# An adaLN block with a long convolution and a gated MLP on one core: one order of accumulation, two stores, one weight form and one activation form moved

## The chip, the cores and the metric

The kernel runs on one core of a Trainium2 chip. Its engines are TensorE (PE in the profile; PEld is its weight loading), VectorE (DVE), ScalarE (ACT), GpSimd (POOL) and SyncE (SP), which here only issues DMAs. ACT issues DMAs too. Each engine runs its own instructions in the order in which the program gives them, and waits on semaphores for the others. The metric is the device time of one execution in microseconds (us).

## The reference

Sequence length S = 2048, width D = 448, hidden width F = 1792, batch 1, all float32.

```python
mod = (silu(c) @ w_mod).reshape(1, 6, 1, -1)          # sa, ca, ga, sb, cb, gb
h = layernorm(q) * (1 + ca) + sa
k_shift = causal_conv4(k, shift_k)                    # per channel
kv = k_shift * v
y = irfft(rfft(kv, 2S) * rfft(ssm_k, 2S))[:S] + kv * ssm_D
x = q + ga * (h * y)
h = layernorm(x) * (1 + cb) + sb
x = x + gb * ((sigmoid(h @ w_gate) * (h @ w_up)) @ w_down)
```

## The kernel before

The first 160 us or so do the long convolution as matrix products, the first normalisation and the gates. Nothing there is touched. The rest is the gated MLP, and it is bound by TensorE.

**Split numbers.** Every operand of a product is split in a high part (the float32 value rounded to the matmul's format, `fp32r`, by a copy on ACT) and a low part (the remainder, by a subtraction on DVE). A product is taken as high·high + low·high + high·low. So each weight form, each activation form and each hidden block costs one ACT instruction and one or two DVE instructions, in this order.

**Rows and hidden groups.** The 2048 rows are four blocks of 512 (n = 0 to 3). The hidden width is seven groups of 256 (k or j = 0 to 6). The gate and up weights of a group come by `load_gu` from DRAM, its down weights by `load_wd`.

**Plain part.** For groups 0 and 1 and row blocks 0 and 1 the products are plain. `plain_half(p, q, n, f)` (L1041 for its matmuls, named gu) makes half a group for a row block: p counts the four pairs (q, n) = (0,0), (1,0), (0,1), (1,1), and f the half. After each half but the first two stands one `down` call, which multiplies the hidden block of the pair before with that group's down weights. Then come the jobs listed in `ends[(p, f)]`. `last_block`, `turn_full` and others run in the middle of a half (`turns`).

**Steps.** After that twelve steps, i = 0 to 11, do the other groups for rows 0 to 1023 and then 1024 to 2047 (and groups 0 and 1 for the latter) with a Strassen-like scheme: seven products per step, with the weight forms A11, S2, S1, S3, A12, A22, S4 (in the order of use) and the activation forms B11, T2, T1, T3, B21, T4, B22. Their matmuls are on L933 (tiles a, b, c in PSUM). Between them stand four `down` calls (`dn`). The second half of the steps (i = 6 and on) works on row blocks 2 and 3.

**Order of the work.** Nothing is planned by a program here: inside the region opened by `tc.manual_schedule()` each engine runs its instructions in the order of the code. A job placed in the lists `ends` or `jobs` (`do("a")`, `do("b")`, … in `step`) stands at that point of the queue of each engine that it uses.

**Names that the change touches.**

- `down(k, n, ks, e)` makes a PSUM tile d from two row tiles (i = 0, 1) with six matmuls each: for each half f of the group (high h, high w), (high h, low w), (low h, high w). The h is the stationary operand. L964 is the matmul, L967 the addition of d to x on DVE. The tile has the tag "y", of which there is one buffer, so the next `down` waits for the addition before it.
- `split_wd_hi` (ACT, L532) and `split_wd_lo` (DVE, L536) make the two parts of the down weights in one of two homes (`wd_of`). `gate_wd` (L526) multiplies them by the gate first. `split_wd_lo` puts the finished pair in the list `kept`.
- `keep_forms(left)` takes stores from that list until `left` remain and issues them on ACT's queue (L543). `w_hi` calls it before its own copy, mostly with `left` = 1. The stored weight forms are read again from step 5 on.
- `w_form` is `w_hi` (ACT, L914) and `w_lo` (DVE, L918); `w_sums` (L894 to L901) makes the sums from the loaded weights on DVE.
- `x_hi` (ACT, L862) and `x_lo` (DVE, L867/L868 or L870) make an activation form in the home that the products read.
- `turn_of` transposes two column tiles of a row block (L851) into a PSUM tile of tag "sa" (one buffer) and copies them out with scale and bias on ACT (`norm_full`, L856). The product tile c of a step has the same tag. `t_sums` (L878 to L885) makes the T sums on DVE from the copied blocks.
- In `step`, u2 (L1209) and u3 (L1216, L1231) are additions on DVE that read the product tiles b and c. b is added to further after u2 has read it.

The part of `step` between the first product and the third, for steps other than 1:

```python
            do("a")
            dn(*((1, 0) if first else (0, 0)))
            lo(0)
            if i < 5 and i != 2:
                gate_wd(JS[i], DVE)
            do("b")
            pb_ = two("t", f"b{i}")
            use(pb_, "S2", "T2", True, True)
            free(2)
            DVE.tensor_add(u2, pb_, c1)
            do("c")
```

Of the kernel before, what the change touches and what calls it, by code (L numbers as in the profile page):

```python
# [79 lines left out]
def adaln_conv_glu_kernel(ctx: ExitStack, tc: tile.TileContext, q, kT, v, ssm, shift, dskip,  # L80
                          wgu, wd, cvec, wmod, c1t, w2t, wat, wbt, out):
    nc = tc.nc
    PE, ACT, DVE, POOL = nc.tensor, nc.scalar, nc.vector, nc.gpsimd
# [11 lines left out]
    late = {}  # L95

    def two(tag, name):

        return ps.tile([P, 2, 512], F32, tag=tag, bufs=2 if tag == "t" else 1, name=name)

    def rows(t):
        return t[:, :, :D]
# [282 lines left out]
    def gate(h, i, y, eng):  # L385

        gg = gt[h, i]
        eng.tensor_mul(pairs(gg), pairs(gg), y)
        gate_add(h, i, gg, eng)
# [57 lines left out]
    def ln2_stats(*tiles, act=()):  # L447

        for i in tiles:
            if i in act:  # L450
                t = two("sa", f"sq{i}")[:, 0, :D] if i > 7 else late["tmp"][:, 29 * C + 32:31 * C + 32]
                ACT.activation(t, x1[:, i], AF.Copy, scale=1.0 / D, accum_out=mv[:, i, 0:1])
                ACT.activation(t, x1[:, i], AF.Square, bias=mv[:, i, 0:1], scale=-1.0, accum_out=mv[:, i, 1:2])
            else:
                st6 = keep.tile([P, nc.vector.BN_STATS_DIM], F32, tag=f"st{i % 2}", name=f"st{i}")
                DVE.bn_stats(st6, x1[:, i])  # L456
                DVE.bn_aggr(mv[:, i], st6)
# [70 lines left out]
    def wd_of(k):  # L528
        return ring["wdk"][k % 2]
# [423 lines left out]
    def down(k, n, ks, e, last=False, split=False, tag="y"):  # L953

        w = wd_of(k)
        g = 4 * n + 2 * e
        pt = two(tag, f"d{k}_{g}")
        for i in range(2):
            ops = []
            for f in range(2):  # L960
                hh, hl = [a1h[ks[f]][:, s] for s in range(2)]
                ops += [(hh, w[:, 0, f]), (hh, w[:, 1, f]), (hl, w[:, 0, f])]
            for m, (h, x) in enumerate(ops):
                PE.matmul(pt[:, i, :D], h[:, (2 * e + i) * P:(2 * e + i + 1) * P], x, start=m == 0, stop=m == len(ops) - 1)  # L964
        for a, b in ((0, 1), (1, 2)) if split else ((0, 2),):
            y = x1[:, g + a:g + b]
            DVE.tensor_add(y, y, rows(pt)[:, a:b])  # L967
            if last:
                nc.sync.dma_start(out[:, g + a:g + b], y)
# [101 lines left out]
    act_stats = lambda *k: ln2_stats(*k, act=k)  # L1071
    do = lambda f, *k, **w: lambda: f(*k, **w)
# [8 lines left out]
    def last_block():  # L1081
# [11 lines left out]
    turns = {(0, 0): last_block, (1, 0): do(turn_full, 1, 0, 1), (1, 1): do(turn_full, 1, 2, 3)}  # L1093
    ends = {(0, 1): [do(split_wd_lo, 0, 0), do(gate_wd, 1, DVE), do(gate, 1, 2, yc[1], DVE)],
            (1, 0): [lambda: gate(1, 3, yc[2], DVE), do(split_wd_hi, 1, 1), do(split_wd_lo, 1, 1), do(load_wd, 2, wdraw), do(load_raw, 2)],
            (1, 1): [do(gate_add, 0, 2, late["g02"], DVE), do(gate_add, 0, 3, late["g03"], DVE), new_xt, do(act_stats, 8, 9), do(t_sums, 1, 2)],
            (2, 0): [do(act_stats, 10, 11, 12), do(w_sums, 2), do(t_sums, 3, 4)],
            (2, 1): [do(x_form, "T2"), do(w_sums, 1, 3, 4), do(act_stats, 13, 14, 15)],
            (3, 0): [do(w_form, "A11", 0), do(load_gu, 3, 2, 6), do(w_form, "S2", 1), do(x_form, "T1"), do(x_hi, "T3")],
# [2 lines left out]
    for p, (q, n) in enumerate(((0, 0), (1, 0), (0, 1), (1, 1))):  # L1102
        for f in range(2):
            plain_half(p, q, n, f, turns.get((p, f)))
            if prev is not None:
                down(prev[0], prev[1], SL[(p - 1) % 2], f, tag="sa" if p == 3 and f else "y")
            for job in ends.get((p, f), []):
                job()
        prev = q, n
# [12 lines left out]
    def step(i, h, jobs):  # L1122
# [23 lines left out]
        def dn(n, e):  # L1146
            down(i + 1, pn0 + n, (h["h11"], h["h21"]) if n == 0 else (h["h12"], h["h22"]), e, i in (5, LAST + 1))
# [172 lines left out]
        else:  # L1320
# [2 lines left out]
        do("i")  # L1323
        return new

    jobs = {0: {"0": [do(w_form, "A12", 4), do(w_form, "A22", 5), do(load_gu, 3, 0, 2)], "a": [do(w_form, "S4", 6)]},
            1: {"a": [do(stats_end, 2, 3)], "c": [do(stats_end2, 2, 3), do(norm_rows, 2), do(dup, ACT)], "f": [do(turn_of, 2, 0, 1, tag="t")]},
            2: {"f": [do(turn_of, 2, 2, 3, tag="t")], "h": [do(norm_rows, 3, (0, 1))]},
            3: {"a": [do(norm_rows, 3, (2, 3))], "b": [do(dup, ACT)], "f": [do(turn_of, 3, 0, 1, tag="t")]},
            4: {"a": [do(x_hi, "B11")], "b": [do(x_lo, "B11"), do(turn_of, 3, 2, 3)], "c": [do(t_sums, 1, 2)], "d": [do(t_sums, 3)], "e": [do(x_hi, "T2")],  # L1330
                "f": [do(x_lo, "T2"), do(x_hi, "T1")], "g": [do(x_lo, "T1"), do(t_sums, 4), do(x_hi, "T3")], "h": [do(x_lo, "T3")]},
            5: {"a": [do(x_hi, "B21")], "b": [do(x_lo, "B21"), do(x_hi, "T4")], "c": [do(x_lo, "T4")], "d": [do(x_hi, "B22")], "e": [do(x_lo, "B22")]}}
    hs = {"h12": 0, "h22": 3, "h11": 1, "h21": 2}
# [2 lines left out]
    for n, ks in ((0, ("h11", "h21")), (1, ("h12", "h22"))):  # L1336
        for e in range(2):
            down(LAST + 2, 2 + n, [hs[k] for k in ks], e, True, n == e == 1, ("y", "t", "t", "sa")[2 * n + e])
# [51 lines left out]
```

## Time and profile before

| | us |
|---|---|
| median of 3 runs | 563.71 (563.62 to 563.82) |
| profiled execution, device time | 563.42 |
| its span in the profile | 561.6 |
| PE busy | 543.6 (97%) |
| DVE busy | 444.4 (79%) |
| ACT busy | 281.6 (50%) |

The views used below are these. The page's first section gives busy time by engine. The view of waits lists for whom an engine sat idle. The timeline gives instructions in order of time: start in us from the span's start, duration in us (of the whole run of equal instructions, if several are merged), engine, line, operation, output and inputs, count, and in brackets the idle time before it with what ended it. "PEld" rows are weight loads; "ACTq" and "SPq" rows are DMA issues. The view by windows gives, for each stretch, its length, busy time and count of PE, PEld, DVE, ACT and POOL, then the clock of PE, the DMA engines' share and GB/s.

### The profile page before, as it was taken

Reading aid. Unit: us, or ns where it says so; the run is one execution under the profiler, and the core shown is the slowest. Engines: PE = TensorE matmul, PEld = TensorE weight load, DVE = VectorE, ACT = ScalarE, POOL = GpSimd, SP = SyncE. Lnnn points to the kernel's source line nnn. Section 1 sums busy time; section 2 is a strip of 40 time slices with the busy share of each in tenths; the row PEclk is TensorE's granted clock in tenths of the full one; section 3 lists DMA queues with packets and bytes.
Section 4 is the critical chain, followed back from the end, with each engine's and each line's share of the span. In section 5 each row is a group of like instructions: output and inputs, shape, how many; then the busy total and the mean of one; then the engine's idle time right before and its main releaser. Section 6 shows DMA issues by size and latency. Waiting matters only on the chain.

```text
span 561.6 us, 7813 instructions
## 1 busy us (share of the span) xinstructions
PE 543.6 (97%) x3004; PEld 414.5 (74%) x3004; DVE 444.4 (79%) x528; ACT 281.6 (50%) x492; POOL 57.5 (10%) x52
## 2 busy tenths in 40 slices
PE   7997899999999999999999999999999999999996
PEld 6564532333577888888888888888888888888886
DVE  0899799989889888898998888885555566979564
ACT  4899578983477586276546452422222122424120
POOL 1000006969500000000000000000000000000000
PEclk9999999999999999999999999999999999999999
DMA  8999999798630408494968295776464662220103
GB/s 278 265 266 394 233 274 279 186 240 174 178 109 0 164 1 312 151 371 186 361 235 308 79 366 158 244 254 242 130 203 142 191 229 90 81 99 17 50 0 132
DMA packets 46809, 107.74 MB, mean 192 GB/s; under 512 B 20018, under 2 KB 25140, under 8 KB 45748
## 3 DMA queue, kind: packets, MB, share of 16 engines
q1 hardware_dynamic: 40468, 82.46, 49.3%
q10 hardware_dynamic: 6304, 24.78, 11.2%
q8 instruction: 24, 0.39, 0.3%
q14 instruction: 13, 0.11, 0.1%
HBM read 70.92 MB, written 35.78 MB: 190 GB/s over the span
## 4 chain that ended last, share of the span: by engine, by line
PE 64%; DVE 5%; ACT 2%; issue 1%; DVEq 0%; ACTq 0%
PE d L964 23%; PE b L933 16%; PE c L933 10%; PE a L933 10%; PE gu L1041 4%; PE pt L851 1%; DVE h L945 1%; ACT xn L833 0%; DVE x L967 0%; DVE xn L831 0%; ACT full L856 0%; DVE wd L536 0%; DVE ring L556 0%; DVE st L456 0%; DVE ring L918 0%
## 5 line engine op out<-in xcount | busy, mean ns | idle before, releaser
L964 PE MATMUL d<-wd,h 128*128 128x448 f32 x672 | 145.6, 366 | 0.6 <-DVE wd L536 0.5
L964 PEld LDWEIGHTS d<-wd,h 128*128 128x128 f32 x672 | 125.8, 188 | 13.6 <-DVE wd L536 1.4
L933 PE MATMUL b<-xt,ring 128*128 128x512 f32 x408 | 99.0, 391 | 0.0
L933 PEld LDWEIGHTS b<-xt,ring 128*128 128x128 f32 x408 | 76.5, 188 | 14.9 <-ACT wd L532 0.2
L967 DVE TENSOR_TENSOR x<-x,d 128x896 f32<-128x896 f32 (+1 forms) x57 | 60.7, 1068 | 17.9 <-PE d L964 17.9
L933 PE MATMUL a<-x,ring 128*128 128x512 f32 x264 | 63.8, 389 | 0.0
L933 PEld LDWEIGHTS a<-x,ring 128*128 128x128 f32 x264 | 49.6, 188 | 10.2
L942 ACT ACTIVATE h<-st 128x512 fp32r<-128x512 f32 x55 | 34.6, 629 | 31.4 <-DVE st L951 19.0
L945 DVE TENSOR_TENSOR h<-st,h 128x512 fp32r<-128x512 f32 x55 | 37.8, 688 | 12.5 <-ACT h L942 12.2
L948 ACT ACTIVATE st<-st 128x512 f32<-128x512 f32 x24 | 15.2, 632 | 63.8 <-DVE st L1278 36.0
L1041 PE MATMUL gu<-x,ring 128*128 128x512 f32 x176 | 42.5, 394 | 0.4 <-ACT full L856 0.4
L1232 ACT ACTIVATE st<-st 128x512 f32<-128x512 f32 x12 | 7.6, 631 | 68.0 <-DVE st L1231 68.0
L1041 PEld LDWEIGHTS gu<-x,ring 128*128 128x128 f32 x176 | 32.7, 188 | 7.9 <-ACT full L856 0.8
L321 DVE TENSOR_TENSOR m<-s2v,ak 128x896 f32<-128x896 f32 x32 | 33.4, 1089 | 3.9 <-PE s2v L317 2.9
L183 DVE STREAM_TRANSPOSE av<-av 128x896 f32<-128x896 f32 x18 | 33.2, 1887 | 2.3 <-ACT av L232 2.3
L933 PE MATMUL c<-x,ring 128*128 128x512 f32 x144 | 34.8, 390 | 0.0
L914 ACT ACTIVATE ring<-sum 128x512 fp32r<-128x512 f32 x28 | 17.2, 626 | 31.7 <-DVE sum L895 16.8
L317 PE MATMUL s2v<-av,w 64*64 64x448 f32 x256 | 31.8, 546 | 1.0 <-DVE av L183 0.5
L933 PEld LDWEIGHTS c<-x,ring 128*128 128x128 f32 x144 | 27.0, 188 | 5.2
L933 PE MATMUL c<-xt,ring 128*128 128x512 f32 x120 | 29.2, 389 | 0.0
L338 PE MATMUL sa<-m,wa 128*64 128x448 f32 x128 | 27.4, 552 | 0.1
L933 PEld LDWEIGHTS c<-xt,ring 128*128 128x128 f32 x120 | 22.5, 188 | 4.6
(184 smaller groups left out, 774.6 us busy)
## 6 DMA issues: line engine op xcount, KB each, us to landing
fd<-ring ACTq DMA_DIRECT2D x35, 512.0 KB
ring<-fd SPq DMA_DIRECT2D x35, 512.0 KB
wdk<-wd ACTq DMA_DIRECT2D x7, 896.0 KB
wd<-wdk SPq DMA_DIRECT2D x7, 896.0 KB
inb<-in_wgu_dram SPq DMA_DIRECT2D x6, 1024.0 KB
kdk<-ak SPq DMA_DIRECT2D x4, 896.0 KB
ak<-kdk SPq DMA_DIRECT2D x16, 224.0 KB
x<-in_q_dram SPq DMA_DIRECT2D x4, 896.0 KB
```

Source lines behind the costliest of these rows:

```text
L183: DVE.transpose(x, x)
L317: PE.matmul(pts[b][c:c + 64, ex, :D], w2[r:r + 64, ex], x[r:r + 64, b], start=True, stop=True)
L321: DVE.tensor_mul(cols4(m[b], h, n), cols4(rows(pts[b]), h, n), k[:, b].unsqueeze(1).to_broadcast([P, 2, D // w, w]))
L338: PE.matmul(y, wa[:, b, r], m[b][:, ex], start=True, stop=True)
L914: ACT.activation(forms[name, i][:, 0], w_src(name), AF.Copy)
L933: PE.matmul(pt, wh(s, t), x[:, k], start=start and m == 0, stop=stop and m == len(ops) - 1, skip_group_check=True)
L942: ACT.activation(hh, h, AF.Copy)
L945: DVE.tensor_sub(hl, h, hh)
L948: ACT.activation(y[:, 0], y[:, 0], AF.Sigmoid)
L964: PE.matmul(pt[:, i, :D], h[:, (2 * e + i) * P:(2 * e + i + 1) * P], x, start=m == 0, stop=m == len(ops) - 1)
L967: DVE.tensor_add(y, y, rows(pt)[:, a:b])
L1041: PE.matmul(pt[:, g], plain(q, t)[:, s, g, f * P:f * P + P], xf[xs_[b]][:, k], start=m == 0, stop=m == 10, skip_group_check=True)
```

## The change

Four places in the order of work are edited. No instruction is added or removed, and the results differ only by the order of one accumulation.

1. `down` with k = n = 0 (the two calls for group 0, rows 0 to 511) runs its six matmuls in the order high·high and low·high of both halves first, and the two with low weights last.
2. `keep_forms` stands also in the jobs after the second half of pair (1, 0), `ends[(1, 1)]`, ahead of `act_stats(8, 9)`. With `left` = 0 it issues the stores of both down-weight pairs of groups 0 and 1, which before were issued by the calls in the forms "A11" and "S2" after `ends[(3, 0)]` begins.
3. In step 0 the form "S4" is made at "c" (behind u2) and not at "a" (ahead of the first `down`).
4. In step 4 (the fifth), `x_hi("B11")` goes from "a" to "b", behind `turn_of(3, 2, 3)`, whose blocks are so copied out first; `x_lo("B11")` goes from "b" to "c", behind u2.

```diff
             for f in range(2):
                 hh, hl = [a1h[ks[f]][:, s] for s in range(2)]
                 ops += [(hh, w[:, 0, f]), (hh, w[:, 1, f]), (hl, w[:, 0, f])]
+            if k == n == 0:
+                ops = [ops[m] for m in (0, 2, 3, 5, 1, 4)]
...
-            (1, 1): [do(gate_add, 0, 2, late["g02"], DVE), do(gate_add, 0, 3, late["g03"], DVE), new_xt, do(act_stats, 8, 9), do(t_sums, 1, 2)],
+            (1, 1): [do(gate_add, 0, 2, late["g02"], DVE), do(gate_add, 0, 3, late["g03"], DVE), new_xt, keep_forms, do(act_stats, 8, 9), do(t_sums, 1, 2)],
...
-    jobs = {0: {"0": [do(w_form, "A12", 4), do(w_form, "A22", 5), do(load_gu, 3, 0, 2)], "a": [do(w_form, "S4", 6)]},
+    jobs = {0: {"0": [do(w_form, "A12", 4), do(w_form, "A22", 5), do(load_gu, 3, 0, 2)], "c": [do(w_form, "S4", 6)]},
...
-            4: {"a": [do(x_hi, "B11")], "b": [do(x_lo, "B11"), do(turn_of, 3, 2, 3)], "c": [do(t_sums, 1, 2)], "d": [do(t_sums, 3)], "e": [do(x_hi, "T2")],
+            4: {"b": [do(turn_of, 3, 2, 3), do(x_hi, "B11")], "c": [do(x_lo, "B11"), do(t_sums, 1, 2)], "d": [do(t_sums, 3)], "e": [do(x_hi, "T2")],
```

## The prediction

> **What bounds the kernel now.** I read the page's first section, then the waits of TensorE's weight loads from 160 us to the end, then the timeline around each moved instruction.
>
> ```profile
> span 561.6 us, 7813 instructions
> PE 543.6 (97%) x3004; PEld 414.5 (74%) x3004; DVE 444.4 (79%) x528; ACT 281.6 (50%) x492; POOL 57.5 (10%) x52
> 280.00:320.00 40.00, 40.00 (x189) 34.60 (x188) 35.65 (x48) 20.75 (x33) 0.00 (x0) 1.00 0.59 226
> PEld d L964 <- DVE wd L536: 1.4, 2, 0.9
> PEld b L933 <- ACT wd L532: 0.2, 1, 0.2
> ```
>
> The third row is a window of the steps: PE is busy 40.00 of 40 us, at clock 1.00. From the first edited place (177 us) on, the waits list has three places where TensorE waits for data: two for low down weights (L536) and one ahead of a b product. So the end is set by the sum of TensorE's work and these stalls. An edit can win no more than the 1.6 us of these two rows, and it loses whatever new stall it makes. DVE, at 35.65 of 40 us, has little room: the question for each edit is what it does to DVE's order.
>
> **Part 1, the low weights last.** The first `down`:
>
> ```profile
> 177.14 1.08 DVE L536 TENSOR_TENSOR wd<-tmp,wd 128x896 fp32r<-128x896 f32 x1
> 177.42 0.36 PE L964 MATMUL d<-wd,h 128*128 128x448 f32 x1
> 178.28 2.12 PEld L964 LDWEIGHTS d<-wd,h 128*128 128x128 f32 x11 [0.90 <-DVE wd L536]
> 180.62 2.66 PE L1041 MATMUL gu<-x,ring 128*128 128x512 f32 x11
> 184.67 1.08 DVE L967 TENSOR_TENSOR x<-x,d 128x896 f32<-128x896 f32 x1
> 186.29 2.44 PEld L964 LDWEIGHTS d<-wd,h 128*128 128x128 f32 x12
> 186.51 2.60 PE L964 MATMUL d<-wd,h 128*128 128x448 f32 x12
> 188.94 3.35 PE L1041 MATMUL gu<-x,ring 128*128 128x512 f32 x14
> ```
>
> An undisturbed `down` takes 188.94 − 186.51 = 2.43 us by starts, 0.2025 a matmul, and its weight load runs 186.51 − 186.29 = 0.22 ahead of its matmul. The first took 180.62 − 177.42 = 3.20, so its stall costs 0.77. The second matmul waits for the low weights, which end at 177.14 + 1.08 = 178.22. From the load at 178.28, eleven matmuls take 2.34 to the next block, against 11 × 0.2025 = 2.23. A stall thus adds 0.11 behind a load that comes late, where an undisturbed load is 0.22 ahead: the first 0.11 of lateness is free.
>
> With the new order four matmuls run first. The fifth load falls due at 177.42 − 0.22 + 4 × 0.2025 = 178.01, and waits until 178.28. Eight matmuls and the 0.11 then end at 178.28 + 1.62 + 0.11 = 180.01: a gain of 0.61 at this place, 0.16 still lost.
>
> What is late next? DVE's L967, which frees the one y buffer, does not move, because nothing DVE does here waits for TensorE. At 186.29 − 0.61 = 185.68 the next `down` meets L967 ending at 185.75 (0.06 later by semaphore, as 178.22 to 178.28 shows): 0.13 late, of which 0.11 is free. Then:
>
> ```profile
> 199.88 1.08 DVE L967 TENSOR_TENSOR x<-x,d 128x896 f32<-128x896 f32 x1
> 201.15 2.44 PEld L964 LDWEIGHTS d<-wd,h 128*128 128x128 f32 x12
> ```
>
> L967 ends at 200.96, ready at 201.02, only 0.13 ahead of the load at 201.15. With the free 0.11, TensorE can keep about 0.25 of the 0.61. **Term: −0.25**, ends 0 (nothing lasts) and −0.61 (L967 comes early as well).
>
> **Part 2, the two stores.** ACT issues two stores of 896 KB after its hidden-block copy at 190.64, and not at 212.37.
>
> ```profile
> 189.28 0.43 SPq L518 DMA_DIRECT2D inb<-in_wgu_dram  x1
> 190.64 0.63 ACT L942 ACTIVATE h<-st 128x512 fp32r<-128x512 f32 x1 [2.62 <-DVE st L1049]
> 192.00:194.00 2.00, 2.00 (x11) 1.65 (x10) 2.00 (x4) 0.00 (x0) 0.00 (x0) 1.00 1.01 401
> 194.09 0.55 ACT L452 ACTIVATE sq<-x 128x448 f32<-128x448 f32 x1 [2.82 <-DVE x L393]
> 196.00:198.00 2.00, 2.00 (x11) 1.68 (x10) 1.90 (x4) 1.51 (x5) 0.00 (x0) 1.00 0.28 68
> 200.88 0.69 DVE L894 TENSOR_TENSOR sum<-inb 128x512 f32<-128x512 f32 x1
> 211.64 0.69 DVE L1049 TENSOR_TENSOR st<-st,gu 128x512 f32<-128x512 f32 x1 [1.41 <-ACT st L1047]
> 212.37 0.84 ACTq L543 DMA_DIRECT2D wdk<-wd  x2
> ```
>
> On ACT the two issues cost 0.84 in all and fall into its idle 2.82 before 194.09: nothing. At 212.37 they go, where they ran under the copy before them: nothing. The stores now share the DMA engines with the load issued at 189.28, which L894 reads at 200.88. The engines are full at 401 GB/s until about 196.4. From 192.5, when the stores begin to move (an estimate: 1.2 us behind issue), about 1.5 MB of load are left (4.4 us at 340), and the stores add 1.8 MB: 3.3 MB at 400 are done by 200.8, before L894 even if every store went first, and at half each the load lands at 200.0. The trace has no load beside stores at this place, so the ends are 0 and some 1.5 us of lateness; DVE catches its 1.41 idle at 211.64 before TensorE feels it. **Term: 0**, ends 0 and +0.4.
>
> The Trainium skill, "DMA: Bandwidth & Descriptors", section on queues, rings and completion order, speaks against this part: each DMA engine round-robins between the queue rows at packet granularity, so SP's load and ACT's stores would share the engines and the load would slow to half. By that rule the load lands at 200.0 and the sum stays as it is; no row of before shows a load slowed by stores to test it.
>
> **Part 3, form S4 in step 0.**
>
> ```profile
> 226.28 0.69 DVE L918 TENSOR_TENSOR ring<-sum,ring 128x512 fp32r<-128x512 f32 x1 [0.99 <-ACT ring L914]
> 226.88 1.08 DVE L967 TENSOR_TENSOR x<-x,d 128x896 f32<-128x896 f32 x1
> 229.49 1.22 DVE L1209 TENSOR_TENSOR st<-b,st 128x1024 f32<-128x1024 f32 x1
> 230.82 2.13 PEld L933 LDWEIGHTS b<-xt,ring 128*128 128x128 f32 x10 [0.21 <-ACT wd L532]
> 253.70 1.09 DVE x L967
> ```
>
> Before, DVE idles 0.99 for S4's high part and subtracts, and L967 and u2 (L1209) stand behind it. u2 ends at 230.71 and the load of the next b product goes at 230.82, after a wait that the row books on L532, although it is b's read by u2 that has to end. After, L967 and u2 come 0.99 + 0.60 = 1.6 earlier and S4's low part (0.69) stands ahead of u3, long before S4's product. The 0.21 wait goes; of it 0.11 was free. ACT's order is the same but for one form's store, whose issue comes earlier and a second one's later. **Term: −0.05 to −0.1, taken as −0.05.** The chain of waits restarts DVE from TensorE's d at 253.70, so the 1.6 helps nothing behind that, and the second stall on L536, at 272.4, stays.
>
> **Part 4, step 4.** The copies out and the high part trade places on ACT; the low part leaves a gap on DVE and goes behind u2.
>
> ```profile
> 332.25 3.00 PE L933 MATMUL b<-xt,ring 128*128 128x512 f32 x12
> 332.54 1.45 ACT L856 ACTIVATE full<-pt,cols 128x512 f32<-128x512 f32 x2
> 333.79 0.69 DVE L867 TENSOR_TENSOR x<-full,x 64x512 fp32r<-64x512 f32 x1
> 334.49 0.69 DVE L868 TENSOR_TENSOR x<-full,x 128x512 fp32r<-128x512 f32 x1
> 335.09 2.43 PE L933 MATMUL c<-xt,ring 128*128 128x512 f32 x10
> 335.29 1.23 DVE L1209 TENSOR_TENSOR st<-b,st 128x1024 f32<-128x1024 f32 x1
> 336.43 1.22 DVE L878 TENSOR_TENSOR full<-full 128x1024 f32<-128x1024 f32 x1
> 359.26 1.21 DVE L1306 TENSOR_TENSOR st<-st,c 128x1024 f32<-128x1024 f32 x1
> 363.23 1.08 DVE L967 TENSOR_TENSOR x<-x,d 128x896 f32<-128x896 f32 x1
> 364.60 2.44 PEld L964 LDWEIGHTS d<-wd,h 128*128 128x128 f32 x12
> 377.62 1.23 DVE L1278 TENSOR_TENSOR st<-b,st 128x1024 f32<-128x1024 f32 x1 [1.05 <-PE b L933]
> ```
>
> The copies (L856) end at 333.99, 1.1 before c needs their buffer at 335.09. They start when the transposes end, at about 332.3, so with the high part gone from ahead of them they gain nothing: TensorE did not wait here. SP's two small copies behind L856 go no later than before, and the split of down weights behind them on ACT has no reader ahead of L878.
>
> On DVE the low part (0.69 twice, by starts 1.3) filled the time until b was ready for u2 at 335.29. Behind u2, that time is idle and everything from L878 is 1.3 later. From 336.43 to 359.26 I find no DVE start that waits for TensorE; the idle there is for ACT's sigmoids and copies, which wait for DVE themselves. So the 1.3 reaches L1306 and, over its sigmoid and hidden-block split, the L967 at 363.23. This ends at 364.31 now and at 365.6 then; the `down` load at 364.60 needs its y buffer. Spare is 0.29 less 0.06, and 0.11 free: the stall costs 1.3 − 0.34 = **+0.95**. u2 of step 5 follows L967, as late as it, and the next b product waits for that too; TensorE is late by then already, so I add only 0.05 (a choice). **Term: +1.0**, ends 0 (the delay is swallowed on the way) and +1.3 (all of it). Behind it DVE has 1.05 idle at 377.62 and is level again.
>
> **The sum.** −0.25 + 0 − 0.05 + 1.0 = +0.7. The profiled execution took 563.42 (span 561.6 and 1.82 around it), so 564.1 by its own time. It lies 0.29 under the median of 563.71, so I forecast 564.4.
>
> **The rivals.**
>
> The y buffer is no limit: if the DVE delay at L967 in step 5 stays under 0.34, part 4 costs nothing and the sum is −0.3, or −0.65 if part 1 keeps its 0.61: 563.1 to 563.4. Against it stands that I see no idle DVE between L878 and L1306 to absorb 1.3.
>
> Part 1 does not last at all (a `down` add already meets TensorE at 201.15), with the rest as forecast: +0.95 to +1.3, 564.7 to 565.0.
>
> Slower, by the load beside the stores: if L894 is late by more than 1.4 us, ACT's and DVE's chain to the first step shifts and TensorE waits for L967 or u2 in step 0. At 2 us late it costs 0.6, for a sum of +1.3: 565.0. It decides beyond 0.2% from 1.85 us late. For it speaks the full DMA share of 1.01; against it the bound of 200.8 above.
>
> **How the numbers follow.** Within 0.2% (1.13 us either way, about what a measurement of this kernel can tell from no change) lie 562.6 to 564.8. Forecast 0.52, with +0.4 to +1.1; y buffer no limit 0.14, of which 0.04 beyond 0.2%, were the stall at 272.4 to go too; part 1 gone 0.17, of which 0.13 beyond 564.8; load late 0.17, all beyond. So faster 0.04, same 0.66, slower 0.30. The range leaves out the full loss of 1.3 with a late load at the top and the best case at the bottom: 563.2 to 565.2. The likeliest case by itself has 564.1 to 564.8.
>
> **What would show it.** Part 1: the first `down` takes 2.6 us and its load waits under 0.3; the `down` load near 201 waits for L967. Part 2: L894 still follows L967 without idle. Part 3: no wait ahead of the b product near 230.8. Part 4: DVE idle 1.5 before u2 near 335, and a new wait of `down` for L967 of about 1 us near 364.6, absent before. If that wait is absent, the prediction is too high by 1.0; if L894 waits, too low.

## The result and the profile after

The changed kernel takes 565.04 us (median) where the kernel before takes 563.78: a ratio of 1.0022, 95% interval 1.0016 to 1.0027. It is slower by 1.26 us, at the line of 0.2% (the interval takes in both sides of it), in the upper part of the forecast range. The profiled execution took 565.02 us. Lines behind L960 are two higher in the changed file: L966, L969, L1043, L1211, L1308 are the L964, L967, L1041, L1209, L1306 of before.

The page's head, and the waits of TensorE's weight loads from 160 us on, of the changed kernel:

```profile
span 563.2 us, 7814 instructions
PE 544.7 (97%) x3004; PEld 414.4 (74%) x3004; DVE 444.6 (79%) x528; ACT 281.7 (50%) x492; POOL 57.6 (10%) x52
PEld d L966 <- DVE x L969: 2.1, 3, 1.1
PEld d L966 <- DVE wd L536: 0.7, 2, 0.5
```

Before, the list held 1.4 us for low down weights and nothing for the addition x. Now the low weights cost half, the wait ahead of the b product of step 0 is gone (one of 0.22 now stands ahead of the b product of the sixth step), and `down` waits three times for the addition of the `down` before it: near 201, 350 and 366 us. The timeline of the changed kernel at the first `down` and at the one near 201:

```profile
177.87 2.73 PE L966 MATMUL d<-wd,h 128*128 128x448 f32 x12
178.71 1.51 PEld L966 LDWEIGHTS d<-wd,h 128*128 128x128 f32 x8 [0.24 <-DVE wd L536]
180.44 2.68 PE L1043 MATMUL gu<-x,ring 128*128 128x512 f32 x11
200.31 1.08 DVE L969 TENSOR_TENSOR x<-x,d 128x896 f32<-128x896 f32 x1
201.31 0.69 DVE L894 TENSOR_TENSOR sum<-inb 128x512 f32<-128x512 f32 x1
201.45 2.33 PEld L966 LDWEIGHTS d<-wd,h 128*128 128x128 f32 x12 [0.41 <-DVE x L969]
228.47 1.21 DVE L1211 TENSOR_TENSOR st<-b,st 128x1024 f32<-128x1024 f32 x1
```

The first `down` takes 180.44 − 177.87 = 2.57 (forecast 2.6, before 3.20); the `down` near 201 then waits for the addition that ended at 201.39; L894 follows without a wait for its load; u2 of step 0 is 1.0 earlier than before (1.6 was forecast; VectorE is 0.66 late ahead of it, with L945 at 219.29 where before had 218.63). Its timeline in the fifth and sixth steps:

```profile
333.96 1.05 ACT L862 ACTIVATE x<-full 128x1024 fp32r<-128x1024 f32 x1
335.78 1.23 DVE L1211 TENSOR_TENSOR st<-b,st 128x1024 f32<-128x1024 f32 x1 [1.95 <-ACT x L862]
337.04 0.69 DVE L867 TENSOR_TENSOR x<-full,x 64x512 fp32r<-64x512 f32 x1
337.74 0.69 DVE L868 TENSOR_TENSOR x<-full,x 128x512 fp32r<-128x512 f32 x1
338.46 1.22 DVE L878 TENSOR_TENSOR full<-full 128x1024 f32<-128x1024 f32 x1
350.39 2.33 PEld L966 LDWEIGHTS d<-wd,h 128*128 128x128 f32 x12 [0.62 <-DVE x L969]
365.07 1.08 DVE L969 TENSOR_TENSOR x<-x,d 128x896 f32<-128x896 f32 x1
366.20 2.33 PEld L966 LDWEIGHTS d<-wd,h 128*128 128x128 f32 x12 [1.09 <-DVE x L969]
368.75 2.11 PEld L933 LDWEIGHTS b<-xt,ring 128*128 128x128 f32 x10 [0.22 <-issue]
```

DVE idles 1.95 ahead of u2, the low part stands behind it, and the delay runs to the addition at 365.07, 1.84 later than in before. It ends at 366.15 and releases the load at 366.20.

A comparison of TensorE's starts in the two profiles gives the account. Executions differ already at 165 us, ahead of the first edit (0.43 here), so I count from there. The changed kernel's shift is +0.43 at 164.99, −0.18 at 180.62 (0.61 won), +0.18 at 203.81 (0.36 of it lost again), +0.06 behind step 0 at 233.21, +0.54 at 352.39, +1.52 at 367.26 and +1.58 from 369.54 to the end.

### The profile page after: what moved, and what is told of

It reads as the page before. It is cut to its first block, busy times and chain, and to the rows that moved or that the text cites. A ratio compares the mean times of both kernels' runs of the same rounds, so it can differ in the third digit from the quotient of the medians.

```text
span 563.2 us, 7814 instructions
## 1 busy us (share of the span) xinstructions
PE 544.7 (97%) x3004; PEld 414.4 (74%) x3004; DVE 444.6 (79%) x528; ACT 281.7 (50%) x492; POOL 57.6 (10%) x52
## 4 chain that ended last, share of the span: by engine, by line
PE 62%; DVE 7%; ACT 2%; issue 1%; DVEq 0%; ACTq 0%
PE d L966 22%; PE b L933 14%; PE c L933 9%; PE a L933 9%; PE gu L1043 7%; DVE x L969 1%; DVE h L945 1%; PE pt L851 1%; ACT xn L833 0%; DVE st L1280 0%; DVE wd L536 0%; DVE st L951 0%; PE y L374 0%; ACT full L856 0%; DVE ring L918 0%
## 5 line engine op out<-in xcount | busy, mean ns | idle before, releaser
L966 PE MATMUL d<-wd,h 128*128 128x448 f32 x672 | 145.8, 366 | 1.0 <-DVE x L969 0.9
L966 PEld LDWEIGHTS d<-wd,h 128*128 128x128 f32 x672 | 125.5, 188 | 14.9 <-DVE x L969 2.1
L969 DVE TENSOR_TENSOR x<-x,d 128x896 f32<-128x896 f32 (+1 forms) x57 | 60.6, 1066 | 17.9 <-PE d L966 17.9
L945 DVE TENSOR_TENSOR h<-st,h 128x512 fp32r<-128x512 f32 x55 | 37.8, 687 | 12.5 <-ACT h L942 12.2
L1043 PE MATMUL gu<-x,ring 128*128 128x512 f32 x176 | 42.5, 395 | 0.4 <-ACT full L856 0.4
L1043 PEld LDWEIGHTS gu<-x,ring 128*128 128x128 f32 x176 | 32.7, 188 | 8.0 <-issue 0.7
```

The source lines that it names most:

```text
L945: DVE.tensor_sub(hl, h, hh)
L1043: PE.matmul(pt[:, g], plain(q, t)[:, s, g, f * P:f * P + P], xf[xs_[b]][:, k], start=m == 0, stop=m == 10, skip_group_check=True)
```

## The experiments

Theory A is that of the prediction: the low part behind u2 makes VectorE late, and the one y buffer hands this to TensorE. The rivals are that the parts cost only together (B), and that ScalarE's new order, the high part behind the copies, is the cause (C). The edits below are against the kernel before unless said otherwise.

| kernel | median us | beside before | last `down` block start less that of the gu block at 165 us |
|---|---|---|---|
| before | 563.8 | | 547.39 − 164.99 = 382.40 |
| the change | 565.04 | +1.26 | 548.97 − 165.42 = 383.55 |
| the change again | 565.01 | +1.26 | 548.81 − 165.17 = 383.64 |
| part 4 alone | 565.06 | +1.26 | 548.69 − 165.00 = 383.69 |
| low part moved alone | 565.14 | +1.34 | 549.00 − 165.19 = 383.81 |
| high part moved alone | 564.50 | +0.70 | 548.77 − 165.74 = 383.03 |
| parts 1, 2, 3 | 563.37 | −0.43 | 547.40 − 165.18 = 382.22 |
| part 4, T2's low part on GpSimd | 565.18 | +1.43 | 549.30 − 165.43 = 383.87 |
| parts 3, 4 | 565.12 | +1.35 | 548.91 − 165.00 = 383.91 |
| parts 1, 4 | 564.78 | +1.01 | 548.64 − 165.00 = 383.64 |
| parts 2, 4 | 565.05 | +1.28 | 548.47 − 164.89 = 383.58 |
| parts 1, 3 and earlier low weights | 563.07, then 562.96 | −0.68, −0.81 | 546.72 − 165.04 = 381.68; 546.69 − 164.90 = 381.79 |
| the same with the T2 sum later | 563.64 | −0.11 | 547.33 − 165.01 = 382.32 |

The last column is TensorE's time from 165 us to the last `down`, in one execution each. Less the 382.40 of before, it is the loss by TensorE's starts: 1.15 and 1.24 in the two executions of the change, 1.29 for part 4 alone. The intervals of the medians below are some 0.5 us wide to either side, so a difference of 0.2 or 0.4 between two of these kernels is read from the starts and not from the medians.

**Part 4 alone.** The edit is the fourth hunk of the change.

> Part 4 alone, put on the kernel before. Theory A (the low part behind u2 makes VectorE late, and the one y buffer hands that to TensorE): the whole loss of the change is here, +1.4 to +1.6 us, with weight loads of down waiting for the addition before them near 350 us and near 366 us. Rival B (the loss comes from the parts together, part 4 alone finds more room): under +1.0. If u2's late start (0.4 us behind the end of its product in the changed kernel) belongs to the edit and not to that one execution, it is here again.

The ratio is 1.0022 (1.0013 to 1.0031). The loss of 1.26 lies under the +1.4 to +1.6 expected by A and above the +1.0 of B; it is as large as that of the whole change, so B falls. Its timeline:

```profile
335.45 1.23 DVE L1209 TENSOR_TENSOR st<-b,st 128x1024 f32<-128x1024 f32 x1 [1.59 <-ACT x L862]
336.70 0.69 DVE L867 TENSOR_TENSOR x<-full,x 64x512 fp32r<-64x512 f32 x1
337.41 0.69 DVE L868 TENSOR_TENSOR x<-full,x 128x512 fp32r<-128x512 f32 x1
338.13 1.23 DVE L878 TENSOR_TENSOR full<-full 128x1024 f32<-128x1024 f32 x1
350.07 2.32 PEld L964 LDWEIGHTS d<-wd,h 128*128 128x128 f32 x12 [0.27 <-DVE x L967]
364.74 1.08 DVE L967 TENSOR_TENSOR x<-x,d 128x896 f32<-128x896 f32 x1
365.88 2.33 PEld L964 LDWEIGHTS d<-wd,h 128*128 128x128 f32 x12 [1.12 <-DVE x L967]
```

From u2 to L878 it is 338.13 − 335.45 = 2.68 us, where before it was 1.14: the low part costs 1.54 of VectorE's time there, not the 1.3 that I took. u2 itself starts about on time, unlike in the whole change.

**The two halves of part 4.**

```diff
# low part moved alone
-            4: {"a": [do(x_hi, "B11")], "b": [do(x_lo, "B11"), do(turn_of, 3, 2, 3)], "c": [do(t_sums, 1, 2)],
+            4: {"a": [do(x_hi, "B11")], "b": [do(turn_of, 3, 2, 3)], "c": [do(x_lo, "B11"), do(t_sums, 1, 2)],
# high part moved alone (the low part still follows it, ahead of u2)
+            4: {"b": [do(turn_of, 3, 2, 3), do(x_hi, "B11"), do(x_lo, "B11")], "c": [do(t_sums, 1, 2)],
```

> Of part 4 only the low part of B11 moves behind u2; the high part stays at 'a', ahead of the copies. Theory A: VectorE is 1.3 to 1.4 us late from the first T sum on, the loss is +0.95 to +1.05, with u2 itself on time. Rival C (ScalarE's new order is the cause: u2 is held by the high part behind the copies): no loss, within 0.1.

> Of part 4 only the high part of B11 moves behind the copies; the low part follows it, still ahead of u2. Theory A: the low part can't start before the high part ends near 335.0, u2 starts near 336.4, 1.1 us late, and the loss is +0.7 to +0.8. Rival C: the loss is as large as in the whole change, +1.5, since ScalarE's order is the same. Rival D (only the place of the low part counts): none.

The low part alone costs all of it: 1.0022 (1.0013 to 1.0032), +1.34, more than the 1.05 expected at most, by the same undersized term. Its rows show the same 2.68 from u2 to L878:

```profile
335.72 1.22 DVE L1209 TENSOR_TENSOR st<-b,st 128x1024 f32<-128x1024 f32 x1 [1.59 <-ACT wd L532]
338.40 1.22 DVE L878 TENSOR_TENSOR full<-full 128x1024 f32<-128x1024 f32 x1
```

C falls: with ScalarE's order as before the loss is whole. The high part alone costs +0.70, 1.0013 (1.0004 to 1.0023), as theory A had it. D, which expected nothing of it, falls too. Its timeline, in an execution that is 0.75 late from 165 us on:

```profile
334.72 1.05 ACT L862 ACTIVATE x<-full 128x1024 fp32r<-128x1024 f32 x1
335.81 0.69 DVE L867 TENSOR_TENSOR x<-full,x 64x512 fp32r<-64x512 f32 x1 [1.21 <-ACT x L862]
337.12 1.22 DVE L1209 TENSOR_TENSOR st<-b,st 128x1024 f32<-128x1024 f32 x1
```

The low part waits for the high part, and u2 starts 337.12 − 0.75 − 335.29 = 1.1 late. So either half of part 4 makes VectorE late; the copies, which now come first, gave nothing back.

**Relief for VectorE.** Part 4, and one subtraction behind it on GpSimd.

```diff
# with part 4
-                "f": [do(x_lo, "T2"), do(x_hi, "T1")],
+                "f": [do(x_lo, "T2", eng=POOL), do(x_hi, "T1")],
```

> Part 4 alone, and the low part of T2 (1.1 us of VectorE near 350 us) computed on the idle GpSimd. Theory A (VectorE's queue carries the delay to the addition that frees the y buffer): VectorE is only 0.3 to 0.4 us late at that addition, the wait of down in the sixth step nearly goes and the loss falls from +1.2 to between 0 and +0.3. Rival C (ScalarE's order, or the high part, is the cause): the loss stays at +1.2.

It gave no relief: +1.43, 1.0024 (1.0014 to 1.0033). The timeline shows why:

```profile
347.71 2.42 POOL L870 TENSOR_TENSOR xt<-xn,xt 128x1024 fp32r<-128x1024 f32 x1 [194.29 <-ACT xt L862]
348.09 0.69 DVE L1157 TENSOR_TENSOR st<-st,a 128x512 f32<-128x512 f32 x1 [0.74 <-ACT st L1156]
348.69 1.98 DVE L945 TENSOR_TENSOR h<-st,h 128x512 fp32r<-128x512 f32 x1
350.59 1.07 DVE L967 TENSOR_TENSOR x<-x,d 128x896 f32<-128x896 f32 x1
351.72 2.33 PEld L964 LDWEIGHTS d<-wd,h 128*128 128x128 f32 x12 [1.56 <-DVE x L967]
365.25 1.08 DVE L967 TENSOR_TENSOR x<-x,d 128x896 f32<-128x896 f32 x1
```

VectorE's L945, 0.69 everywhere else, took 1.98 while GpSimd's subtraction ran; L1157, which ran in the same time and reads one of its inputs (a) from PSUM, kept its 0.69. What the GpSimd took off VectorE's list behind 350 us it took back ahead of it, and the stall came at 351.72 and not in the sixth step, where the later TensorE no longer waits. The run therefore does not test A by relief. It shows the handing over once more, by the same buffer at the other place.

**Parts 1 to 3.**

> Parts 1 to 3 without part 4. Theory A: -0.35 us (0.25 left of part 1 after the addition near 200 us, 0.1 from part 3), that is 563.4 where before is 563.75. Rival B: parts 1 to 3 share in the loss, at or over the time of before.

By time they gain 0.43, ratio 0.9991 (0.9982 to 1.0001), an interval that takes in no change; by TensorE's starts they gain 0.18. The prediction's terms were −0.30. By time, −0.43 and +1.26 do not add up to the +1.26 of the whole: 0.4 is missing, which the intervals allow. By starts −0.18 + 1.29 = 1.11 stands against 1.15 and 1.24. What the rows do show is that in the whole change u2 of the fifth step starts 0.35 later than in part 4 alone. The next runs went after this.

> The changed kernel once more, for a second profile. In the first its u2 of the fifth step began 0.35 us behind the end of its semaphore wait, in part 4 alone it did not. If that belongs to this program, it is here again and the loss from 165 us on is about 1.15 us by the profile as in the first; if it belongs to one execution, u2 starts within 0.1 us of its wait and the loss from 165 us on is 0.8 to 0.9 us.

> Parts 3 and 4. Part 4 alone cost 1.25 us and parts 1 to 3 alone gained 0.4, but together they cost 1.25, some 0.4 more than the sum; in both profiles of the whole change u2 of the fifth step begins 0.35 us behind the end of its semaphore wait. Part 3 is the only other part that changes VectorE's list (one form moved, some waits more). Theory E: the 0.35 comes with part 3's list, it is here, and the kernel costs +1.4 to +1.5. Theory F (it comes from elsewhere, or the sum was only scatter): u2 begins within 0.1 us of its wait and the kernel costs +1.1 to +1.2.

> Parts 1 and 4. VectorE's list is that of part 4 alone. Theory E: u2 on time, 1.25 for part 4 less 0.25 for part 1, +1.0. Theory F with part 1 as the partner: u2 late by 0.35, +1.3.

> Parts 2 and 4. Part 2 is expected to cost nothing: the weight sums near 201 us start without a wait, and the kernel costs what part 4 alone does, +1.2 to +1.3. If the earlier stores make the weight load late by more than VectorE can give, +1.5 or more; if they take something away later (fewer stores between 212 and 230 us), under +1.1.

The second profile of the change has the late u2 again. So has parts 3 and 4; parts 1 and 4, and parts 2 and 4, don't. The first row is of the change, second execution, the next of parts 3 and 4, the last two of parts 1 and 4 and of parts 2 and 4:

```profile
335.61 1.23 DVE L1211 TENSOR_TENSOR st<-b,st 128x1024 f32<-128x1024 f32 x1 [1.95 <-ACT x L862]
```

```profile
335.67 1.22 DVE L1209 TENSOR_TENSOR st<-b,st 128x1024 f32<-128x1024 f32 x1 [1.95 <-ACT x L862]
```

```profile
335.42 1.23 DVE L1211 TENSOR_TENSOR st<-b,st 128x1024 f32<-128x1024 f32 x1 [1.59 <-ACT x L862]
```

```profile
335.25 1.23 DVE L1209 TENSOR_TENSOR st<-b,st 128x1024 f32<-128x1024 f32 x1 [1.59 <-ACT x L862]
```

The idle time is 1.95 in every kernel with parts 3 and 4, and 1.59 in every kernel with part 4's low part and without part 3. In all of them VectorE's semaphore wait for u2 lasts 3.62 us and ends with the b product; the 0.36 lies between its end and u2's start. So theory E holds as to where it comes from. Why part 3, which changes VectorE's list some 100 us earlier (an order, and a few waits more), delays an instruction here stays open. The DMA view for 325 to 338 us shows one packet on each of two instruction queues in before, in part 4 alone and in the change, so it does not tell them apart.

By TensorE's starts, parts 3 and 4 cost 1.51 against part 4's 1.29; by time it is +1.35, a little under the +1.4 to +1.5 that theory E expected. The effect is clearest from the `down` at 300.69 us of before on, where part 4 alone is left to act. From there to the last `down` (547.39 − 300.69 = 246.70 in before) the loss is 1.50, 1.51 and 1.54 in the two executions of the change and in parts 3 and 4. It is 1.20, 1.24, 1.17 and 1.17 in part 4 alone, with its low part alone, in parts 1 and 4 and in parts 2 and 4. So part 3 makes part 4 dearer by about 0.3. Part 2 costs nothing that can be told: parts 2 and 4 cost 1.28, part 4 alone 1.26.

Parts 1 and 4 show something else. Without part 3, part 1 keeps nothing in the profiled execution. Their timeline in step 0:

```profile
229.54 1.22 DVE L1211 TENSOR_TENSOR st<-b,st 128x1024 f32<-128x1024 f32 x1
230.87 2.14 PEld L933 LDWEIGHTS b<-xt,ring 128*128 128x128 f32 x10 [0.39 <-ACT wd L532]
```

TensorE comes to the b product 0.2 earlier than in before, u2 does not, and the wait grows from 0.21 to 0.39: the shift goes from −0.16 at 203.81 to +0.05 at 230.85. With part 3, u2 is early enough and the gain stays. Part 3 needs no partner for its own gain: in parts 3 and 4 the shift goes from +0.05 at 203.81 to −0.06 at 233.21. The medians do not bear out the loss of part 1's gain: parts 1 and 4 took 0.25 less than part 4 alone (+1.01 against +1.26), as theory E expected, where the starts say 1.24 against 1.29. The intervals overlap, so this rests on the rows of one execution.

**A faster version.** Parts 1 and 3, and the other stall on L536 (272.4 us) taken up by VectorE's order in step 1.

```diff
             glu(c1, [lambda: lo(4), lambda: lo(5)])
             do("f")
-            sums_of(4)
-            load_gu(JS[i + 2], 0, 2)
+            split_lo()
             dn(1, 1)
             finish_h(new["h21"], c1[:, 0])
-            split_lo()
+            sums_of(4)
+            load_gu(JS[i + 2], 0, 2)
             hi(2)
```

> Parts 1 and 3, without 2 and 4, and in step 1 the low down weights (L536, which end at 272.4 us where the weight load of the next down is due at 271.8) are made ahead of the addition of down and of the S4 sum, not behind them. If the second stall on L536 is VectorE's order alone, it goes: 0.35 from parts 1 and 3 and 0.4 from this, -0.75 us together. If the addition that is now later holds the y buffer, the stall only changes its name: -0.35.

> Parts 1 and 3 with the low down weights of step 1 made earlier, timed in more rounds: -0.65 us as before, whose interval lay between -0.05% and -0.24%.

563.07 and, timed again, 562.96: −0.68 and −0.81, ratio 0.9985 (0.9976 to 0.9995) and 0.9984 (0.9975 to 0.9992). The stall is gone and did not change its name:

```profile
268.80 1.09 DVE L536 TENSOR_TENSOR wd<-wdraw,wd 128x896 fp32r<-128x896 f32 x1
269.80 1.08 DVE L969 TENSOR_TENSOR x<-x,d 128x896 f32<-128x896 f32 x1
271.45 2.44 PEld L966 LDWEIGHTS d<-wd,h 128*128 128x128 f32 x12
```

The low weights end at 269.89, 2.5 earlier, the addition at 270.88, and the load at 271.45 waits for neither. It beats both kernels.

```diff
# on top of that
-            (1, 1): [..., new_xt, do(act_stats, 8, 9), do(t_sums, 1, 2)],
-            (2, 0): [do(act_stats, 10, 11, 12), do(w_sums, 2), do(t_sums, 3, 4)],
+            (1, 1): [..., new_xt, do(act_stats, 8, 9), do(t_sums, 1)],
+            (2, 0): [do(act_stats, 10, 11, 12), do(w_sums, 2), do(t_sums, 2, 3, 4)],
```

> As the kernel before it, and the T2 sum (1.65 us of VectorE near 196 us) is made one half later, beside T1's and T4's sums. The addition that capped part 1 near 200 us then comes 0.35 us earlier, so 0.25 us more of part 1 would last: -1.0 us together. If VectorE then is late near 208 us, where it had 1.4 us idle at 211.6 to give, the gain is lost again there: -0.75 or less.

The hoped-for −1.0 did not come, 563.64, −0.11: the addition near 200 did come earlier, and the next one gave back all of part 1's gain and more. The load at 209.09 is booked on a ScalarE row, but the addition, which ends at 208.98, is the one that releases the matmul.

```profile
200.73 2.33 PEld L966 LDWEIGHTS d<-wd,h 128*128 128x128 f32 x12 [0.17 <-DVE x L969]
207.90 1.08 DVE L969 TENSOR_TENSOR x<-x,d 128x896 f32<-128x896 f32 x1
209.09 2.32 PEld L966 LDWEIGHTS d<-wd,h 128*128 128x128 f32 x12 [1.08 <-ACT sq L452]
209.13 2.67 PE L966 MATMUL d<-wd,h 128*128 128x448 f32 x12 [0.69 <-DVE x L969]
```

## Why the prediction was right or wrong

**Part 1, right.** 0.61 was forecast at 180 us and measured; 0.25 was to be left behind the addition near 201, and 0.25 was left at 203.81 (+0.43 to +0.18). What the prediction did not say is that this 0.25 needed part 3 to pass step 0: the profile of parts 1 and 4 shows it lost at 230.85.

**Part 2, right in its term, not in its working.** ACT's issues fell into its idle time, and L894 did not wait. But the load had little of the company that the prediction gave it. The issue of the stores and two DMA windows of the changed kernel (the last two columns are the share of the engines and GB/s):

```profile
191.14 1.05 ACTq L543 DMA_DIRECT2D wdk<-wd  x2
200.00:202.00 2.00, 2.00 (x10) 1.40 (x9) 2.00 (x3) 1.91 (x7) 0.00 (x0) 1.00 0.94 392
202.00:204.00 2.00, 2.00 (x12) 1.85 (x11) 1.82 (x2) 1.94 (x7) 0.00 (x0) 1.00 0.08 32
```

And its DMA view by queue (packets, MB, share of the engines), the first row for 190 to 196 us, the next two for 196 to 198; q1 carries SP's transfers, q10 the stores:

```profile
q1 hardware_dynamic: 254, 1.81, 98.3%
q10 hardware_dynamic: 61, 0.44, 51.9%
q1 hardware_dynamic: 51, 0.26, 33.4%
```

The engines are busy until about 202, against the 200.8 of the estimate (this execution is 0.4 late throughout). But the stores, issued at 191.14, moved nothing before 196; the prediction had them begin 1.2 us behind their issue. By 198 SP's queue had moved 2.07 MB, and the 0.23 MB that it moved later is less than the two small copies of 128 KB behind the load. So the load was done by 198, and not at 200.0 as by half its rate. The small copies were the last: a T sum waited 0.15 for them. The rival of a late load did not come, and with the load ahead of the stores for most of its time this run hardly tests it. Why the stores began so late stays open; before, with no load in the way, they were issued at 212.37 and moved from 213.2 on.

**Part 3, right in size, incomplete.** Its 0.1 in step 0 is there (+0.18 to +0.06). It has a second effect, the 0.36 at u2 of the fifth step, which no step of the prediction held.

**Part 4, right in its mechanism and place, too small.** The failing step is "by starts 1.3" for the low part. The prediction does not say how it came about; 0.70 from L867 to L868, and 0.60, as behind S4's low part in part 3's rows (226.28 to 226.88), make it, with nothing for the step into it. Behind u2, 1.25 passes from u2 to L867 instead of the 1.14 to the next instruction before, 0.71 to L868 and 0.72 to L878: 1.54. With the prediction's own room of 0.34 this gives 1.20, and part 4 alone measured 1.26 by time and 1.29 by TensorE's starts. With the 0.36 that part 3 adds it gives 1.56; the changed kernel lost 1.52 between 233.21 and 369.54. The formula held, two of its sizes did not. In part 4 alone 1.41 of the 1.54 reached the addition (364.74 − 363.23 = 1.51, less 0.10 that this execution was late at 300 us), and the b product behind it added 0.10 where the prediction chose 0.05. The prediction also missed that the `down` near 350 would wait; this cost no more in the end, because the load near 366 is released by the addition, whenever TensorE arrives.

The sum: −0.25 + 0 − 0.05 + 1.0 was forecast. By TensorE's starts it was −0.25 (part 1), −0.12 (part 3) and +1.52 (part 4 with part 3's 0.36), +1.15, and by time +1.26. The likeliest case's own range, to +1.1, just missed it. Two rivals had the time, near 565.0, and not the cause: a late load, and part 1's gain gone. That the time lies in the forecast range is owed to these rivals, and so in part to luck.

The size could have been read in before, from the same pair of instructions in the sixth step:

```profile
356.72 1.22 DVE L885 TENSOR_TENSOR xn<-full,xn 128x1024 f32<-128x1024 f32 x1
357.95 0.69 DVE L867 TENSOR_TENSOR xt<-full,xt 64x512 fp32r<-64x512 f32 x1
358.65 0.69 DVE L868 TENSOR_TENSOR xt<-full,xt 128x512 fp32r<-128x512 f32 x1
```

L867 starts 1.23 behind L885, 0.09 more than the 1.14 from u2 to L878, L868 follows 0.70 behind, and L1306 0.61 behind that: 1.40 in all.

The dearer low part has an explanation that agrees with the rows, though no run varied it. The third of the three steps, to L878, is a wait by the code: T1's sum overwrites the block that L868 reads. For the first two, the Trainium skill, "VectorE: DVE Perf Modes", section on two Vector instructions with no wait between them, says that an instruction whose operands start in another group of 32 partitions than those before it is held until all earlier ones have finished. L867 works on 64 partitions only, the upper half by the code (`o[64:128, 1]`). In part 4's rows it starts 336.70 − 335.45 = 1.25 behind u2, whose duration is 1.23, and L868 follows 0.71 behind, at a duration of 0.69. An instruction that isn't held starts some 0.1 before the end of the one ahead of it, as L878 did in the kernel before (1.14 behind a u2 of 1.23).

## What to carry to other kernels

A job moved out of an engine's waiting time into its busy time costs its whole length, and more where it breaks the overlap of neighbours; follow the delay along the engine's queue to the first single buffer that another engine waits for, and subtract only the room there. A gain on the bound engine lasts only as far as the next engine that runs at its own pace: here one reordering kept 0.25 of 0.61 at one buffer, and kept that only with a second edit further on. Edits need not add up: by TensorE's starts part 1 kept its gain only beside part 3, and part 3 made part 4 dearer by 0.3.

## What the runs showed of the hardware

An idle GpSimd is no free help for VectorE: a 2.42 us subtraction on GpSimd, which VectorE does in 1.22, stretched one VectorE instruction from 0.69 to 1.98 us, which ended 0.54 behind it. The Trainium skill, "SBUF — State Buffer", section "SBUF: two separate sides", says that a VectorE instruction with two inputs in SBUF and a GpSimd instruction that reads SBUF exclude each other for a whole instruction; the row agrees, since L945 has both inputs there.

A reordering on VectorE near 226 us delayed one instruction at 335 us by 0.36 us, in all three profiles that had it beside part 4 and in none of the five with part 4's low part and without it. The semaphore wait had ended; the profile names nothing for the rest.

A store can wait long behind its issue: with a load of 1536 KB in progress on SP's queue, two stores issued by ACT at 191.14 us moved nothing before 196 us, where with no load in progress they began 0.9 us behind their issue. The cause was not looked for.
